# One more pair of token tiles through Strassen's algorithm in the output projection of a fused attention and gated feed-forward kernel

## Chip, cores and metric

The kernel runs on one core of one Trainium2 chip. The metric is the device time of one launch in microseconds (us), as the median of several runs; lower is better. TensorE is written PE (its weight loads PEld), VectorE DVE, ScalarE ACT, GpSimd POOL, and SyncE SP, which here only issues DMAs.

## What is computed

Windowed attention with a few global keys and a linear bias, then a feed-forward layer with a ReLU gate. Cut to what matters:

```python
scores = q @ k.T / sqrt(64) - slope[h] * dist        # 4 batches, 8 heads, 768 tokens, head size 64
a = softmax(where(is_global | is_local, scores, -1e9))    # 8 global keys, a window of 96
x = (a @ v)                                          # as 3072 tokens x 512
h = maximum(x @ w_gate, 0) * (x @ w_val)             # 512 -> 1536
out = h @ w_out                                      # 1536 -> 512, float32
```

## The kernel before

The 3072 tokens are worked in eight halves of 384 (a half is half a batch), numbered c = 0 to 7. A half's 384 tokens are three tiles of 128. For each half there are three kinds of work:

- **Attention** (`attention_pieces`): score matmuls into four PSUM banks at a time (`score_unit`, L513), the exponential on ACT (`unit_exp`, L522), a product with a mask table on DVE (L534, es times m_all, both bf16 in SBUF; it is emitted one piece later than its exponential, or at the next `flush`), the product with the values on PE (`piece_av`, L431, once for each of two heads of a pair: e = 0 and e = 1), then on ACT a logarithm (L440) and after the second head an exponential (L445) that make the reciprocal of the row sum, and on DVE a multiplication for each head that writes the normalised result to xT (`piece_norm`, L451). `N` below is the second of these two multiplications.
- **First projections** (`gate` and `val` in `ffn_pieces`): for each of 12 blocks of 128 hidden columns four matmuls of 128x384 with w_gate and four with w_val (both L741). ACT applies the ReLU to the gate's bank (L750), and DVE multiplies the val bank by it and writes ht, in fp16 (L757).
- **Output projection**: either `single(n)`, a tile by itself in four parts of three matmuls 128x512 with the weights wo_sb (`outp`, L774), with a copy to obuf on ACT (L779) and a store from SP (L780); or a `Pair`: two tiles with Strassen's algorithm. A pair makes seven products of six matmuls 128x256 (L632) where two single tiles need 24 matmuls of 128x512. It needs four sums of ht blocks (`sums`, L625 to L628, DVE, written to hsum), four differences of wo_sb blocks in wo_sum (`weight_sums`, L598), which are made once for all pairs, a copy of 128x256 on ACT (L659), four additions on DVE from PSUM into obuf (L643), and two stores (L652).

A bank for gate, val, a single tile or a pair's products comes from one pool of three (`ff_psum`), handed out in turn: the matmuls of a bank wait until the reader of the bank three before it is done. Attention's banks come from two other pools.

Half 0 and half 1 start together. Their attention and the first two thirds of their hidden columns are worked in an order written out by hand. The stage that the change touches comes after it (L990 to L993). It is one list of steps: the last four gate and val blocks of half 0 (steps 1 to 8), the same of half 1 (steps 9 to 16), half 0's three tiles as singles (steps 17 to 28), half 1's third tile as a single with the four sums of its pair behind its four parts (steps 29 to 32), and half 1's pair in seven products named p1, p2, p4, p6, p5, p7, p3 (steps 33 to 39). `weave` walks through this list and puts other pieces between the steps. Each step counts 0.65, and a piece with a fraction f is emitted after the first step at which the steps so far have reached f times the total. `spread` gives a list of pieces equal distances between two fractions. Three lists are spread here: the attention of half 2 over 0.02 to 0.86, the early pieces of half 3 over 0.1 to 0.76 (casts of k and q on POOL, L367; transposes as DMAs from SP, L372; copies that order the keys on POOL), and the eight weight differences over 0.42 to 0.76. Every engine works through its own instructions in the order in which they were emitted.

From half 2 on, each half is a stage of its own with the next half's attention woven in, and its first two tiles are a pair. The weights w_out are loaded with one DMA from POOL's queue before the stage (L923).

Of the kernel before, what the change touches and what calls it, by code (L numbers as in the profile page):

```python
# [16 lines left out]
def kernel(  # L17
# [88 lines left out]
    def w_of(t, dc, fc):  # L106
        f = fc % GW
        return t[fc // GW][:, dc, f * 128 : (f + 1) * 128]
# [269 lines left out]
    def early_pieces(s):  # L378
        out = [(0.0, lambda p=p: piece_cast2(s, p, kc, ks_of)) for p in range(HP)]
        out += [(0.0, lambda n=n: piece_x(kNb[s % 2], kc[s % 2], n)) for n in range(NN)]  # L380
        out += [(0.0, lambda p=p: piece_cast2(s, p, qc, qs_of)) for p in range(HP)]
        out += [(0.0, lambda n=n: piece_x(qT2[s % 2], qc[s % 2], n)) for n in range(NN)]
        out += [(0.0, lambda p=p: piece_order(s, p)) for p in range(HP)]
        return out
# [156 lines left out]
    def attention_pieces(s):  # L541
        masks, units = [], []

        def flush():
            for f in masks:
                f()
            masks.clear()

        def scores(groups, pools):
            units.extend(score_unit(s, groups, list(pools)))  # L550

        def x(scored=None):
            ready = masks[:]
            masks.clear()
            if scored:
                scores(*scored)
            masks.append(unit_exp(s, *units.pop(0)))
            for f in ready:
                f()

        U = [([(0, 0), (0, 1)], (AVB, QKB, QKB, QKB)),
             ([(0, 2), (1, 0)], (AVB, QKB, QKB, QKB)),
             ([(1, 1), (1, 2)], (AVB, QKB, QKB, QKB))]
        X = lambda u=None: [(0.0, lambda: x(u))]
        AV = lambda p: [(0.0, lambda e=e: (flush(), piece_av(s, p, e))) for e in range(2)]
        N = lambda p: [(0.0, lambda: piece_norm(s, p, 1))]
        wait = [(0.0, lambda: None)]
        a0, a1 = AV(0), AV(1)

        return (X(U[0]) + X() + X() + X() + wait + X(U[1]) + X() + X() + a0[0:1] + X() + a0[1:2] + N(0) + wait  # L570
                + X(U[2]) + X() + a1[0:1] + X() + X() + a1[1:2] + N(1) + wait * 2 + AV(2) + N(2) + wait * 2
                + AV(3) + N(3))
# [11 lines left out]
    NP = N_FC // 2  # L584
# [8 lines left out]
    def weight_sums(i0, i1):  # L593
        b = lambda f, d: B(i0, i1, f, d)
        t = lambda n: T(n, i0, i1)
        for out_, x, y in ((t(1), b(0, 1), b(0, 0)), (t(2), b(1, 1), t(1)),
                           (t(4), b(1, 0), t(2)), (t(3), b(1, 1), b(0, 1))):
            yield lambda o=out_, x=x, y=y: nc.vector.tensor_tensor(o, x, y, op=ALU.subtract)  # L598
# [132 lines left out]
    def ffn_pieces(c):  # L731
        ht_of[c] = ht = ht_pool.tile([128, N_FC, QH], FP16, name="ht")
        st = {}
        pair = Pair((c, 0), (c, 1))
        first = {}

        def products(key, w, fc, d0, d1):
            if d0 == 0:
                st[key] = ff_psum.tile([128, 512], FP32, name="ff_ps")
            for dc in range(d0, d1):  # L740
                nc.tensor.matmul(st[key][:, 0:QH], lhsT=w_of(w, dc, fc), rhs=xT_of[c][:, dc, :],  # L741
                                 start=(dc == 0), stop=(dc == N_DC - 1))
            return st[key]

        def gate(fc, d0=0, d1=N_DC):
            psg = products(f"g{fc % 4}", wg, fc, d0, d1)
            if d1 < N_DC:
                return
            gr = gr_pool.tile([128, QH], BF16, name="grelu")
            nc.scalar.activation(gr, psg[:, 0:QH], AF.Relu, bias=0.0, scale=1.0)  # L750
            st["r", fc] = gr

        def val(fc, d0=0, d1=N_DC):
            psv = products("v", wv, fc, d0, d1)
            if d1 < N_DC:
                return
            nc.vector.tensor_tensor(ht[:, fc, :], psv[:, 0:QH], st["r", fc], op=ALU.mult)  # L757

            if c > 1 and 7 <= fc < N_FC - 1:
                if fc == 7:  # L760
                    first[0] = pair.sums(0, 4)
                first[0][fc - 7]()

        f1 = []
        for fc in range(N_FC):
            f1.append((0.65, lambda *d, fc=fc: gate(fc, *d)))
            f1.append((0.65, lambda *d, fc=fc: val(fc, *d)))

        def outp(n, part, after):
            if part == 0:  # L770
                st["o"] = ff_psum.tile([128, DM], FP32, name="ff_ps")
            ps2 = st["o"]
            for fc in range(part * NP // 2, (part + 1) * NP // 2):
                nc.tensor.matmul(ps2, lhsT=ht[:, fc, n * 128 : (n + 1) * 128], rhs=wo_sb[:, fc, :],  # L774
                                 start=(fc == 0), stop=(fc == N_FC - 1))
            if part == 3:
                osb = obuf[:, n_results[0] % 2, 0:2]
                n_results[0] += 1
                nc.scalar.copy(osb, ps2)  # L779
                nc.sync.dma_start(out=out_v[c, n], in_=osb)  # L780
            for f in after:
                f()

        def single(n, *after):
            after = after or ((),) * 4
            return [(0.65, lambda part=part: outp(n, part, after[part])) for part in range(4)]

        if c == 0:
            return f1, single(0) + single(1) + single(2)
        late = pair.sums(0 if c == 1 else 4, NP)  # L790
        if c == 1:
            return f1, single(2, *([f] for f in late)) + pair.items()
        if c < NHALF - 2:
            return f1, single(2, [], [], [], late[0:2]) + pair.items({"1": late[2:4]})
        if c == NHALF - 2:
            return f1, pair.items({"1": late[0:2], "2": late[2:4]})

        space = qTb[0].rearrange("d p e t -> d (p e t)").bitcast(FP16)
        across = Pair((c - 1, 2), (c, 2), space.rearrange("t (s c z) -> t s c z", s=4, c=NP))
        sums = across.sums(0, NP)  # L800
        return f1, (pair.items({"1": late[0:2], "2": late[2:4], "4": sums[0:1], "6": sums[1:2], "5": sums[2:4]})
                    + across.items(split=True))


    def spread(items, first, last):

        n = len(items)
        return [(first + (i + 0.5) / n * (last - first), f) for i, (_, f) in enumerate(items)]
# [17 lines left out]

    V, P, A = nc.vector, nc.gpsimd, nc.scalar
    f1_0, f2_0 = ffn_pieces(0)
    f1_1, f2_1 = ffn_pieces(1)
    G = [slice(2 * GW * i, 2 * GW * (i + 1)) for i in range(N_FC // GW)]  # L830
    F0 = [f for _, f in f1_0]
# [147 lines left out]
    def T2_piece(p):  # L979
# [10 lines left out]
    sums_wo = [(0.0, f) for i in (0, 3) for f in weight_sums(i, i + 3)]  # L990
    weave(f1_0[G[2]] + f1_1[G[2]] + f2_0 + f2_1,
          spread(attention_pieces(2), 0.02, 0.86), spread(early_pieces(3), 0.1, 0.76),
          spread(sums_wo, 0.42, 0.76))  # L993

    for c in range(2, NHALF):
        placed = []
        if c + 1 < NHALF:
            placed.append(spread(attention_pieces(c + 1), 0.0, 0.92 if c + 2 < NHALF else 0.87))
        if c + 2 < NHALF:
            load_qk(c + 2, 0, H)  # L1000
            load_v_half(c + 2)
            placed.append(spread(early_pieces(c + 2), 0.25, 0.75))
        f1, f2 = ffn_pieces(c)
        weave(f1 + f2, *placed)
# [35 lines left out]
```

The softmax here doesn't subtract the row's maximum and nothing guards it: scores larger than these inputs give would overflow.

## Time and profile before

| what | value |
|---|---|
| median of 7 runs | 239.17 us (238.59 to 239.9) |
| the profiled execution | 239.37 us, of which the span from the first to the last instruction is 237.6 us |
| PE busy over the span | 230.9 us (97%), granted clock 1.00 |
| DVE, ACT, POOL busy | 174.3 us, 149.3 us, 89.2 us |
| matmuls 128x384 (L741) | 768, mean 326 ns |
| matmuls 128x512 (L774) | 96, mean 378 ns |
| matmuls 128x256 (L632), all groups | 336, median 273 ns |
| the stage of the change | 46.63 to 75.95 us |

A matmul's duration holds its way through the array, and the next one starts before it ends; what a matmul takes from PE's time is the distance from one start to the next. The same holds in part for DVE and ACT, where a following instruction that waits for nothing starts some 0.08 us before the end of the one before. In a timeline a row gives the start, the time that the merged instructions take together, the engine, the line, what is written and read, and how many instructions the row merges; in brackets stands the idle time before it and what ended that.

### The profile page before, as it was taken

The page shows a single profiled execution, that of the slowest core. Times are in us where ns is not written, and L with a number is a line of the kernel's source. Part 1 is how long each engine was busy: PE and PEld are TensorE (multiplying, and loading weights), DVE is VectorE, ACT ScalarE, POOL GpSimd, SP SyncE. Part 2 cuts the span into 40 slices and gives each one's busy share as a digit, 9 for nine tenths or more (in the row PEclk, how much of TensorE's full clock was granted, in tenths as well). Part 3 has the DMA queues.
Part 4 walks back from the last instruction along what each step waited for, and adds up shares of the span by engine and source line. Part 5 has one row for each costly group of instructions (what it writes and reads, how often), then busy time and mean ns, then how long its engine had stood idle before and what let it go on. Part 6 is the DMA issues. An engine that isn't in the chain of part 4 may idle for free.

```text
span 237.6 us, 5381 instructions
## 1 busy us (share of the span) xinstructions
PE 230.9 (97%) x1967; PEld 152.8 (64%) x1967; DVE 174.3 (73%) x442; ACT 149.3 (63%) x324; POOL 89.2 (38%) x191
## 2 busy tenths in 40 slices
PE   8899999999999999999999999999999999999993
PEld 4675766656558566766658666675658566766682
DVE  6877767756778689486867879576876878864783
ACT  7999856577653787557764787547764787523300
POOL 8998904924295066402492063701550000000000
PEclk9999999999999999999999999999999999999999
DMA  6999999998369943919349666649431200020004
GB/s 180 193 174 185 205 277 267 169 102 261 79 189 122 286 130 90 97 59 296 68 73 126 195 192 89 62 84 289 104 70 44 91 0 0 3 88 0 3 8 170
DMA packets 70650, 30.42 MB, mean 128 GB/s; under 512 B 47744, under 2 KB 69248, under 8 KB 70624
## 3 DMA queue, kind: packets, MB, share of 16 engines
q0 software_dynamic: 34896, 10.27, 38.4%
q1 hardware_dynamic: 35728, 19.82, 29.2%
q8 instruction: 15, 0.25, 0.4%
q14 instruction: 11, 0.09, 0.1%
HBM read 28.38 MB, written 6.29 MB: 146 GB/s over the span
## 4 chain that ended last, share of the span: by engine, by line
PE 84%; POOL 7%; DMA 4%; issue 1%; DVE 1%; ACT 0%; DVEq 0%; POOLq 0%
PE ff_ps L741 50%; PE ff_ps L632 15%; PE ff_ps L774 9%; PE av_ps L431 6%; DMA wv<-in_moe_w_val_dram 4%; POOL vbuf L154 3%; PE av_ps L513 2%; PE qk_ps L513 2%; POOL kc L131 1%; POOL wg L171 1%; POOL qT L195 1%; PE qk_ps L299 1%; DVE xT L451 0%; POOL wv L171 0%; POOL vbuf L141 0%
## 5 line engine op out<-in xcount | busy, mean ns | idle before, releaser
L741 PE MATMUL ff_ps<-xT,wv 128*128 128x384 bf16 x384 | 77.9, 326 | 0.1
L741 PE MATMUL ff_ps<-xT,wg 128*128 128x384 bf16 x384 | 77.9, 326 | 0.0
L750 ACT ACTIVATE grelu<-ff_ps 128x384 bf16<-128x384 f32 x96 | 46.7, 489 | 48.0 <-PE ff_ps L741 34.8
L757 DVE TENSOR_TENSOR ht<-ff_ps,grelu 128x384 f16<-128x384 f32 x96 | 53.3, 556 | 27.1 <-PE ff_ps L741 23.4
L741 PEld LDWEIGHTS <-wv 128*128 128x128 bf16 x384 | 36.0, 98 | 23.9 <-issue 1.1
L741 PEld LDWEIGHTS <-wg 128*128 128x128 bf16 x384 | 36.3, 98 | 22.0 <-issue 0.7
L451 DVE TENSOR_TENSOR xT<-av_ps,rcp 64x384 bf16<-64x384 f32 x48 | 26.6, 555 | 20.9 <-ACT rcp L445 19.8
L440 ACT ACTIVATE lnd<-av_ps 64x384 f32<-64x384 f32 x48 | 23.3, 485 | 16.0 <-PE av_ps L431 15.2
L534 DVE TENSOR_TENSOR es<-es,m_all 128x432 bf16<-128x432 bf16 (+3 forms) x108 | 30.9, 329 | 0.7 <-ACT es L522 0.7
L367 POOL CAST kc<-ks 128x384 bf16<-128x384 f32 x20 | 10.0, 542 | 55.3 <-DMA ks<-in_k_dram 47.7
L522 ACT ACTIVATE es<-qk_ps 128x432 bf16<-128x432 f32 (+2 forms) x54 | 27.8, 531 | 0.1
L154 POOL DMA_DIRECT2D vbuf<-in_v_dram x29 | 24.7, 861 | 0.3 <-DVE ht L757 0.3
L774 PE MATMUL ff_ps<-wo_sb,ht 128*128 128x512 f16 x96 | 23.6, 378 | 0.0
L431 PEld LDWEIGHTS <-vbuf 128*128 128x128 bf16 x216 | 18.3, 98 | 6.6
L643 DVE TENSOR_TENSOR obuf<-ff_ps,obuf 128x512 f32<-128x512 f32 (+1 forms) x34 | 20.0, 594 | 3.1 <-PE ff_ps L632 0.8
L431 PE MATMUL av_ps<-es,vbuf 128*128 128x216 bf16 (+4 forms) x216 | 21.4, 226 | 0.0
L632 PEld LDWEIGHTS <-hsum 128*128 128x128 f16 x168 | 16.3, 98 | 1.8
L632 PEld LDWEIGHTS <-ht 128*128 128x128 f16 x144 | 13.8, 98 | 2.9 <-DVE ht L757 0.4
L632 PE MATMUL ff_ps<-wo_sum,hsum 128*128 128x256 f16 x126 | 14.9, 272 | 0.0
L774 PEld LDWEIGHTS <-ht 128*128 128x128 f16 x96 | 8.6, 97 | 8.0 <-issue 0.6
L445 ACT ACTIVATE rcp<-lnd 128x384 f32<-128x384 f32 x24 | 12.6, 523 | 0.8
L632 PE MATMUL ff_ps<-wo_sb,ht 128*128 128x256 f16 x96 | 12.1, 273 | 0.1
(130 smaller groups left out, 254.1 us busy)
## 6 DMA issues: line engine op xcount, KB each, us to landing
out_dram<-obuf SPq DMA_DIRECT2D x22, 256.0 KB
ks<-in_k_dram SPq DMA_DIRECT2D x5, 768.0 KB
qs<-in_q_dram SPq DMA_DIRECT2D x5, 768.0 KB
vbuf<-in_v_dram POOLq DMA_DIRECT2D x23, 120.0 KB, 4.7
wv<-in_moe_w_val_dram POOLq DMA_DIRECT2D x3, 512.0 KB, 10.0
wo_sb<-in_moe_w_out_dram POOLq DMA_DIRECT2D x1, 1536.0 KB, 21.1
wg<-in_moe_w_gate_dram POOLq DMA_DIRECT2D x2, 512.0 KB, 10.0
ks<-in_k_dram SPq DMA_DIRECT2D x4, 192.0 KB
```

Source lines behind the costliest of these rows:

```text
L154: nc.gpsimd.dma_start(out=v_dst(b, NG + r0, NG + r0 + n, j), in_=v[b, :, KT * j + r0 : KT * j + r0 + n, :].rearrange("h p d -> p h d"))
L431: nc.tensor.matmul(av3[:, :, a : a + w], lhsT=vb[:, j, z0 : z0 + 128], rhs=es[:, c : c + NN * w].rearrange("k (n p) -> k n p", n=NN), star ...
L440: nc.scalar.activation(ln[o0 : o0 + 64], av[d0 : d0 + 64, 0:QH], AF.Ln, bias=0.0, scale=1.0)
L451: nc.vector.tensor_tensor(xT_of[s][r, p, :], av_of[s, p, e][r, 0:QH], av_of[s, p, "r"][r], op=ALU.mult)
L522: nc.scalar.activation(es[:, 0:cols], ps[:, 0:cols], AF.Exp, bias=0.0, scale=scale)
L534: nc.vector.tensor_mul(e4, e4, mk)
L632: nc.tensor.matmul(ps[:, c0 : c0 + DH], lhsT=lhs(i), rhs=rhs(i), start=(i == 0), stop=(i == NP - 1), skip_group_check=True)
L643: add = lambda o, x, y: nc.vector.tensor_tensor(o, x, y, op=ALU.add)
L741: nc.tensor.matmul(st[key][:, 0:QH], lhsT=w_of(w, dc, fc), rhs=xT_of[c][:, dc, :], start=(dc == 0), stop=(dc == N_DC - 1))
L750: nc.scalar.activation(gr, psg[:, 0:QH], AF.Relu, bias=0.0, scale=1.0)
L757: nc.vector.tensor_tensor(ht[:, fc, :], psv[:, 0:QH], st["r", fc], op=ALU.mult)
L774: nc.tensor.matmul(ps2, lhsT=ht[:, fc, n * 128 : (n + 1) * 128], rhs=wo_sb[:, fc, :], start=(fc == 0), stop=(fc == N_FC - 1))
```

## The change

Half 0's first two tiles are now a pair as well. Its list of steps is its third tile as a single, with the four sums of the pair behind its four parts, and then the seven products. The weight differences that this pair needs are spread over 0.08 to 0.4 of the stage instead of 0.42 to 0.76, among the gate and val steps. The stage has 38 steps instead of 39. Nothing else is touched.

```diff
@@ ffn_pieces
-        if c == 0:
-            return f1, single(0) + single(1) + single(2)
-        late = pair.sums(0 if c == 1 else 4, NP)
-        if c == 1:
+        late = pair.sums(0 if c < 2 else 4, NP)
+        if c < 2:
             return f1, single(2, *([f] for f in late)) + pair.items()
@@ the stage of halves 0 and 1
     weave(f1_0[G[2]] + f1_1[G[2]] + f2_0 + f2_1,
           spread(attention_pieces(2), 0.02, 0.86), spread(early_pieces(3), 0.1, 0.76),
-          spread(sums_wo, 0.42, 0.76))
+          spread(sums_wo, 0.08, 0.4))
```

## Prediction

> **What bounds the kernel now.** I read the page first: which engine fills the span, and what the chain that ended last is made of.
>
> ```profile
> PE 230.9 (97%) x1967; PEld 152.8 (64%) x1967; DVE 174.3 (73%) x442; ACT 149.3 (63%) x324; POOL 89.2 (38%) x191
> ...
> PEclk9999999999999999999999999999999999999999
> ...
> PE 84%; POOL 7%; DMA 4%; issue 1%; DVE 1%; ACT 0%; DVEq 0%; POOLq 0%
> ```
>
> TensorE is the bound at full clock, and hardly anything else is on the chain after the start. So matmul time taken out is gained, unless PE has to wait. Next, the stage of the change, 46.63 to 75.95 us. PE's timeline gives the price of each kind of matmul:
>
> ```profile
> 58.08 0.81 PE L741 MATMUL ff_ps<-xT,wv 128*128 128x384 bf16 x4
> ...
> 59.36 1.47 PE L774 MATMUL ff_ps<-wo_sb,ht 128*128 128x512 f16 x6
> 60.66 0.42 PE L431 MATMUL av_ps<-es,vbuf 128*128 128x216 bf16 x4
> ...
> 71.37 1.47 PE L632 MATMUL ff_ps<-wo_sb,ht 128*128 128x256 f16 x12
> 72.67 0.82 PE L632 MATMUL ff_ps<-wo_sum,ht 128*128 128x256 f16 x6
> ...
> 75.95 0.81 PE L741 MATMUL ff_ps<-xT,wg 128*128 128x384 bf16 x4
> ```
>
> From start to start: six 128x512 take 1.30 us (0.217 each), twelve 128x256 take 1.30 (0.108 each), the 42 of a pair 71.37 to 75.95, or 4.58 (0.109 each). A gate or val step is 0.65 us, an av piece (L431) 0.28. The steps add up to the stage's 29.32 us, so PE has almost no gap in it. The DVE timeline of the stage shows how near the gaps are:
>
> ```profile
> 50.08 0.56 DVE L757 TENSOR_TENSOR ht<-ff_ps,grelu 128x384 f16<-128x384 f32 x1 [0.72 <-PE ff_ps L741]
> 50.55 0.67 DVE L534 TENSOR_TENSOR es<-es,m_all 128x432 bf16<-128x432 bf16 x2
> 51.38 0.56 DVE L757 TENSOR_TENSOR ht<-ff_ps,grelu 128x384 f16<-128x384 f32 x1 [0.16 <-PE ff_ps L741]
> ...
> 58.30 0.55 DVE L451 TENSOR_TENSOR xT<-av_ps,rcp 64x384 bf16<-64x384 f32 x1 [1.21 <-ACT rcp L445]
> 58.77 0.54 DVE L757 TENSOR_TENSOR ht<-ff_ps,grelu 128x384 f16<-128x384 f32 x1
> 59.33 0.56 DVE L451 TENSOR_TENSOR xT<-av_ps,rcp 64x384 bf16<-64x384 f32 x1
> 59.92 0.56 DVE L757 TENSOR_TENSOR ht<-ff_ps,grelu 128x384 f16<-128x384 f32 x1
> 60.39 0.51 DVE L534 TENSOR_TENSOR es<-es,m_all 128x432 bf16<-128x432 bf16 x1
> 60.83 0.55 DVE L598 TENSOR_TENSOR wo_sum<-wo_sb 128x768 f16<-128x768 f16 x1
> ```
>
> The ht at 58.77 is step 14's (half 1's third val block of four). It ends at 59.31, and step 17, the first output step, starts at 59.36: it takes the bank three further on, so it needs that very ht. This has 0.05 us of room already.
>
> **The change part by part.**
>
> *Matmuls.* 24 x 0.217 = 5.20 us go, 4.58 come: 0.62 us less PE work. The rest of the stage from step 17 on was 75.95 - 59.36 = 16.59 us and becomes 15.97, if nothing waits.
>
> *The eight differences move from behind step 17 into steps 4 to 15.* One lasts 0.55 us; behind each other they start 0.47 apart (70.95, 71.42, 71.89, 72.36 for one difference and three sums of ht, same shape). Between 50.08 and 57.60 DVE is busy 4.96 of 7.52 us, with none of them. Six now fall in there: 6 x 0.47 = 2.82 us into 2.56 us of room. By the fractions, DVE's order after ht of step 4 is: mask 2, difference 1, mask 3, ht of step 6, difference 2, mask 4, difference 3, ht of step 8, mask 5, difference 4, mask 6, ht of step 10, mask 7, difference 5, ht of step 12, difference 6, mask 8, first normalisation, difference 7, second normalisation, ht of step 14. The last pair matters most: 38 steps instead of 39 move the second normalisation (fraction 0.342) from behind step 14 to behind step 13, so it and difference 7 now stand ahead of step 14's ht.
>
> Starts, with 0.47 for an ht or a difference, 0.33 for a mask (0.35 for masks 5 and 6, which are two instructions each): ht 50.08, difference 1 50.88, ht of step 6 51.68, ht of step 8 53.42 (its bank is ready at 53.25, as before), ht of step 10 55.06, ht of step 12 56.33 (ready 56.13), difference 6 56.80, mask 8 57.27, first normalisation 57.60. Its reciprocal is ready by then: the second av piece comes after step 12, at 55.86 instead of 56.51, and the logarithm and the exponential end at about 57.4. Then difference 7 at 58.07 (0.47), second normalisation 58.64 (0.57, as 69.31 to 69.88), ht of step 14 at 59.23 (0.59, as 59.33 to 59.92), end 59.79; 0.06 us later PE can start (58.85 to 58.91 is the same step from DVE to PE): 59.85. PE would have been there at 59.31. Everything after it stands behind this wait on PE, so the whole rest of the kernel moves by it. DVE never idles in between, so no wait further up changes this end. Cheapest case: were the differences shorter, the reciprocal would still hold the chain at 57.46, which gives 59.71.
>
> *Contention with POOL.* From 56.77 on POOL runs eight casts, which hang on a load and not on this change:
>
> ```profile
> 56.77 2.04 POOL L367 CAST kc<-ks 128x384 bf16<-128x384 f32 x4 [7.59 <-PE ff_ps L741]
> 58.81 1.86 POOL L367 CAST qc<-qs 128x384 bf16<-128x384 f32 x4
> ```
>
> Difference 6, mask 8 and difference 7 fall into them; all three read two SBUF operands. The trace has no difference beside a cast, but masks beside casts, in a later stage:
>
> ```profile
> 165.43 0.70 DVE L534 TENSOR_TENSOR es<-es,m_all 128x432 bf16<-128x432 bf16 x1
> ...
> 167.00 0.63 DVE L534 TENSOR_TENSOR es<-es,m_all 128x432 bf16<-128x432 bf16 x1
> ```
>
> An undisturbed one takes 0.37. Five such masks beside casts took 0.51 (60.39), 0.49 (111.51), 0.42 (113.08), 0.70 and 0.63: 0.05 to 0.33 us more, 0.18 in the mean. A difference beside POOL's key copies took 0.82 instead of 0.55. The Trainium skill (SBUF — State Buffer, "Who interferes with whom") has a stricter rule that speaks against this change: a VectorE instruction with two SBUF inputs and a GpSimd instruction that reads SBUF exclude each other for a whole instruction. By it each of the three could lose a whole cast, 0.51 us: 1.53 together. By the rows it is 3 x 0.18 = 0.54. I take the rows' mean, since they are the same pair of operations, and keep 0.15 and 1.53 for the range; below nothing it can't go, as the casts and these instructions stay the same work. Step 17 then starts at 59.85 + 0.54 = 60.39, or 1.03 us later than before.
>
> *The sum.* 1.03 - 0.62 = +0.41 us.
>
> *What I cost at nothing.* ACT loses two copies of 0.58 and gains one of 0.35. DVE gains four sums (0.47 each) and four additions (three of 0.69, one of 0.42) behind step 17, and seven differences have left there, so it stays at some 14 of 16 us. Worked on in order, the last sum of ht is done near 64, and the first product that reads one ends near 66.2; the additions that free the bank for half 1's single end near 67.7, and it starts near 68.7. That is 1 us of cover; beyond it PE waits one for one. The differences read w_out: that load was issued at 25.74 and took 21.1 us, so it landed near 46.8, 4 us before the first of them. On SP two stores of 256 KB are replaced by two of the same size; one stands ahead of the q transposes instead of three among them. Those ended near 69 and are needed at 76.7. What SP or ACT might gain or lose there is off PE's path.
>
> The profiled execution took 239.37 us with its span of 237.60, 1.77 around it, and the median is 0.20 lower. The sum is a difference within the span; I put it on the median: 239.17 + 0.41 = 239.6.
>
> **Rivals.**
>
> 1. *The saving arrives whole.* DVE absorbs the differences, step 17 starts at 59.31: -0.05 - 0.62 gives 238.5. For it: DVE is idle a third of that window. Against it: the 0.05 us of room, and the second normalisation's new place, which delays step 14's ht even if the differences cost nothing. Chance 0.10.
> 2. *The port decides, and the kernel is slower.* Difference 6, mask 8 and difference 7 each lose 0.33 (the worst row) to 0.51 us (a whole cast), because instructions of 0.55 us back to back always meet the next cast. Step 17 starts at 60.84 to 61.38, +0.86 to +1.40: 240.0 to 240.6. It decides from 0.29 us lost per instruction on. For it: the row of 0.82 beside key copies, and the skill's rule. Against it: most rows of masks. Chance 0.27.
> 3. *The pair doesn't take less PE time*, because 256 wide matmuls are held by their weight loads (98 ns under 109): near 240.2. Half 1's pair at 0.109 each speaks against it. Chance 0.03.
>
> The forecast itself, a wait at step 17 between 0.40 and 1.3 us, gives -0.27 to +0.7 and has 0.60.
>
> **How the numbers follow.** Likeliest: 239.6. The low end, 238.8, lies just under the cheapest case of the forecast (239.17 - 0.27 = 238.9) and leaves out rival 1. The high end, 240.5, reaches through nearly all of rival 2. A measurement here tells about 0.3% (0.7 us) from no change. Faster by more: half of rival 1, 0.05. Slower by more: rivals 2 and 3, 0.30. Within: 0.65.
>
> **What would show it.** In the changed profile: 72 matmuls L774 and 378 L632; the differences between 50.9 and 60.4 us; DVE without an idle gap from 50 to 60; the ht ahead of the first L774 ending between 59.7 and 61.3, and before that L774 PE idle with DVE ht L757 as its releaser; L598 or L534 rows stretched beside L367; the stage ending at 76.4 (75.95 before). If the first L774 starts at 59.3, the DVE count is wrong. If PE waits instead for the additions at half 1's single or for the sums of ht, my 1 us of cover was wrong, and the time is above the forecast.

## The result and the profile after

The changed kernel takes 238.3 us (median of 13 runs, 237.91 to 239.34) against 239.19 us (32 runs, 238.59 to 240.06): a ratio of 0.996 [0.995, 0.9971], or 0.9 us less. The forecast was 239.6 with a range from 238.8. The time is that of rival 1, the saving that arrives whole (238.5), though not for the reason that rival 1 gave.

The page of the changed kernel, the engines' busy time, the granted clock and the chain's shares:

```profile
PE 229.5 (97%) x1985; PEld 154.2 (65%) x1985; DVE 177.4 (75%) x450; ACT 148.4 (63%) x323; POOL 89.1 (38%) x191
...
PEclk9999999999999999999999999999999999999999
...
PE 83%; POOL 7%; DMA 4%; DVE 2%; issue 1%; ACT 0%; POOLq 0%; DVEq 0%
```

PE is still the bound at full clock, with 1.4 us less work; DVE has 3.1 us more and still hardly stands on the chain. PE's timeline around the first output step (step 17), at half 1's single and at the stage's end (a row gives start, time, engine, line, what is written and read, count, and in brackets the wait ahead of it, if there is one):

```profile
57.28 0.81 PE L741 MATMUL ff_ps<-xT,wg 128*128 128x384 bf16 x4
57.93 0.81 PE L741 MATMUL ff_ps<-xT,wv 128*128 128x384 bf16 x4
58.67 0.26 PE L513 MATMUL av_ps<-qT,kT 64*128 64x216 bf16 x1
...
59.13 1.47 PE L774 MATMUL ff_ps<-wo_sb,ht 128*128 128x512 f16 x6
...
67.41 1.46 PE L774 MATMUL ff_ps<-wo_sb,ht 128*128 128x512 f16 x6
...
75.12 0.81 PE L741 MATMUL ff_ps<-xT,wg 128*128 128x384 bf16 x4
```

No row of the stage has a bracket: PE waits nowhere, neither at step 17 (59.13) nor at half 1's single (67.41). The stage runs from 46.48 to 75.12, 28.64 us against 29.32 before: 0.68 less. Rival 1 had 0.67. DVE's timeline beside it:

```profile
55.98 0.56 DVE L757 TENSOR_TENSOR ht<-ff_ps,grelu 128x384 f16<-128x384 f32 x1
56.45 0.55 DVE L598 TENSOR_TENSOR wo_sum<-wo_sb,wo_sum 128x768 f16<-128x768 f16 x1
56.92 0.68 DVE L534 TENSOR_TENSOR es<-es,m_all 128x432 bf16<-128x432 bf16 x1
57.52 0.54 DVE L451 TENSOR_TENSOR xT<-av_ps,rcp 64x384 bf16<-64x384 f32 x1
57.99 0.54 DVE L598 TENSOR_TENSOR wo_sum<-wo_sb,wo_sum 128x768 f16<-128x768 f16 x1
58.56 0.56 DVE L451 TENSOR_TENSOR xT<-av_ps,rcp 64x384 bf16<-64x384 f32 x1
59.15 0.56 DVE L757 TENSOR_TENSOR ht<-ff_ps,grelu 128x384 f16<-128x384 f32 x1
```

The order and the lack of gaps are as forecast, and the last row is step 14's ht: it starts at 59.15 and ends at 59.71. But PE started step 17 at 59.13, before that ht had begun. So step 17 does not wait for it. What frees its bank stands in ACT's timeline, the ReLU of step 15's gate, which ends at 58.62, 0.51 us ahead of PE:

```profile
58.13 0.49 ACT L750 ACTIVATE grelu<-ff_ps 128x384 bf16<-128x384 f32 x1 [0.52 <-PE ff_ps L741]
```

The bank lists of two kernels below (`PICKS`), which write out the changed kernel's own order but for one exchange each, say the same: in this stage steps 1 to 16 each take the bank of three requests back, step 17 that of two back (step 15), and the pair's first product after it that of four back (step 14). So the banks are not handed out in turn, as the description of the kernel before has it; why the pool chooses as it does is not shown.

### The profile page after: what moved, and what is told of

The parts are those of the page before. It is cut to its first block, busy times and chain, and to the rows that moved or that the text cites. A ratio compares the mean times of both kernels' runs of the same rounds, so it can differ in the third digit from the quotient of the medians.

```text
span 236.4 us, 5424 instructions
## 1 busy us (share of the span) xinstructions
PE 229.5 (97%) x1985; PEld 154.2 (65%) x1985; DVE 177.4 (75%) x450; ACT 148.4 (63%) x323; POOL 89.1 (38%) x191
## 4 chain that ended last, share of the span: by engine, by line
PE 83%; POOL 7%; DMA 4%; DVE 2%; issue 1%; ACT 0%; POOLq 0%; DVEq 0%
PE ff_ps L741 51%; PE ff_ps L632 16%; PE ff_ps L774 7%; PE av_ps L431 6%; DMA wv<-in_moe_w_val_dram 4%; POOL vbuf L154 3%; PE av_ps L513 2%; PE qk_ps L513 2%; POOL kc L131 1%; DVE obuf L643 1%; POOL wg L171 1%; POOL qT L195 1%; PE qk_ps L299 1%; DVE xT L451 0%; POOL wv L171 0%
## 5 line engine op out<-in xcount | busy, mean ns | idle before, releaser
L757 DVE TENSOR_TENSOR ht<-ff_ps,grelu 128x384 f16<-128x384 f32 x96 | 53.3, 556 | 25.5 <-PE ff_ps L741 23.2
L367 POOL CAST kc<-ks 128x384 bf16<-128x384 f32 x20 | 10.8, 584 | 56.0 <-DMA ks<-in_k_dram 56.0
L643 DVE TENSOR_TENSOR obuf<-ff_ps,obuf 128x512 f32<-128x512 f32 (+1 forms) x38 | 22.6, 597 | 2.4 <-issue 0.5
L632 PEld LDWEIGHTS <-hsum 128*128 128x128 f16 x192 | 18.4, 98 | 2.1
L774 PE MATMUL ff_ps<-wo_sb,ht 128*128 128x512 f16 x72 | 18.0, 378 | 0.0
L632 PEld LDWEIGHTS <-ht 128*128 128x128 f16 x162 | 15.4, 97 | 3.3 <-DVE ht L757 0.4
L632 PE MATMUL ff_ps<-wo_sum,hsum 128*128 128x256 f16 x144 | 17.2, 272 | 0.0
L632 PE MATMUL ff_ps<-wo_sb,ht 128*128 128x256 f16 x108 | 13.9, 272 | 0.1
L522 ACT ACTIVATE es<-av_ps 128x432 bf16<-128x432 f32 (+2 forms) x18 | 9.5, 527 | 2.7 <-PE qk_ps L513 1.8
```

What stands on the lines that cost most here:

```text
L522: nc.scalar.activation(es[:, 0:cols], ps[:, 0:cols], AF.Exp, bias=0.0, scale=scale)
L632: nc.tensor.matmul(ps[:, c0 : c0 + DH], lhsT=lhs(i), rhs=rhs(i), start=(i == 0), stop=(i == NP - 1), skip_group_check=True)
L643: add = lambda o, x, y: nc.vector.tensor_tensor(o, x, y, op=ALU.add)
```

## The experiments

The theory after the result: the saving of 0.67 us arrives because step 17 stands on step 15's bank, and DVE's lag, which came about as forecast, ends in a bank that is needed only at the pair's first product (62.00). The rival: the lag itself is harmless, or was smaller than it seems, whichever bank is taken.

**The bank that the forecast assumed.** The changed kernel with its banks from a written list, in which step 17 gets step 14's bank and the pair's first product that of step 15; nothing else differs.

```diff
-    ff_psum = ctx.enter_context(tc.tile_pool(name="ffps", bufs=3, space=bass.MemoryType.PSUM))
+    ff_banks = [ctx.enter_context(tc.tile_pool(name=f"ffps{i}", bufs=1, space=bass.MemoryType.PSUM)) for i in range(3)]
+    # tile() takes ff_banks[PICKS[n]] for the n-th request
```

> The experiment that the first one meant to be, with the bank exchanged at the right place: the changed kernel, but step 17, half 0's single tile, gets the bank that the ht of step 14 empties, and the step after the single gets the other. Theory A (VectorE fell behind as forecast, and only the bank's owner differs): the first L774 starts 0.06 us after the ht of step 14 ends, 59.77 instead of 59.13 on the changed kernel's clock, and the stage becomes 0.64 us longer, 29.3 instead of 28.64: 238.9 us, ratio to before 0.999. Theory B (the lag is made up within the stage): 238.3 us, 0.996.

PE's timeline of this kernel at step 17, then DVE's (its lines stand 11 further down, so L785 is L774, L768 is L757):

```profile
60.04 1.46 PE L785 MATMUL ff_ps<-wo_sb,ht 128*128 128x512 f16 x6 [0.57 <-DVE ht L768]
```

```profile
59.43 0.56 DVE L768 TENSOR_TENSOR ht<-ff_ps,grelu 128x384 f16<-128x384 f32 x1
```

Now PE waits, 0.57 us, for the ht that ends at 59.99, and starts 0.05 us after it. The stage takes 29.26 us (46.76 to 76.02), 0.62 more than the changed kernel's and 0.06 less than before: the pair's saving is eaten in the place and by the wait that the forecast named. The time is 239.06 us, ratio 0.9979 [0.9967, 0.9991]. The theory holds; the rival falls.

**The same in another stage.** Meant for step 17, this list instead changed the bank of the first output step of half 3, which then gets the bank of the val block three back.

> The changed kernel with one difference: the first output step of the stage (step 17, half 0's third tile) gets the PSUM bank of step 14's val block, which VectorE empties, instead of the bank of step 15's gate block, which ScalarE empties. Theory A (VectorE did fall behind as worked out, and the forecast's wait is missing only because step 17 doesn't have that bank): step 17's first matmul starts 0.06 us after the ht of step 14 ends, at 59.8 instead of 59.1, and all that follows moves by 0.6 us: 238.9 us, ratio to the kernel before 0.999. Theory B (the lag of VectorE would be made up again within the stage, whichever bank is used): no change from the changed kernel, 238.3 us, 0.996.

PE's timeline of this kernel:

```profile
119.68 0.81 PE L752 MATMUL ff_ps<-xT,wv 128*128 128x384 bf16 x4
121.00 0.81 PE L785 MATMUL ff_ps<-wo_sb,ht 128*128 128x512 f16 x3 [0.51 <-DVE ht L768]
```

The stage of the change is as in the changed kernel (28.65 us), and the expected wait is absent there, since that bank was not touched. Where the list did hit, a wait of 0.51 us appears that neither kernel has, and what follows is 0.58 us later. The ratio is 0.9975 [0.9965, 0.9985]. So it tells nothing on step 17, but it shows the same thing at another place: half 3's single tile starts without a wait on the bank that the pool gave it, and with one on the val block's bank.

**The differences alone.** The kernel before, with the eight differences at 0.08 to 0.4 and no new pair.

> The kernel before with only the second part of the change: the eight weight differences at 0.08 to 0.4 of the stage, half 0's tiles still singles. Theory A: the differences cost nothing where they now are and gained nothing by leaving where they were, so 239.2 us, ratio 1.000, with the stage at 29.3 us. Theory C (a part of the gain of 0.89 us beyond the 0.62 us of matmuls comes from moving the differences away from the crowded end of the stage): 238.9 to 239.0 us, ratio 0.999. The theory of the forecast, with the waiting bank three steps back, gives 239.2 to 239.7 here.

239.22 us against 239.27, ratio 1.0001 [0.9988, 1.0014]; the stage takes 29.33 us without a wait on PE. The move by itself costs nothing and brings nothing, so the gain comes with the pair. The run does not test the bank: without the pair's shorter list, step 14's ht still stands ahead of the second normalisation and ends at 59.13, just before PE's 59.17, so whichever bank step 17 takes, hardly anything would wait.

**The differences later.** The changed kernel with them at 0.3 to 0.55 of the stage.

> The changed kernel with the differences at 0.3 to 0.55 of the stage instead of 0.08 to 0.4, about as late as the pair's products allow (the last one of those that the third product reads comes two steps ahead of it). Theory A: now VectorE's lag meets someone who waits: the third product (p4) reads a difference that ends near 64.1 and it would start at 63.6, so PE waits 0.3 to 0.8 us: 238.6 to 239.1 us, ratio 0.998 to 1.000. Theory B (lags on VectorE are made up within the stage): 238.3 us, 0.996.

PE's timeline of this kernel at the first product that reads a difference, then DVE's:

```profile
66.94 0.49 PE L632 MATMUL ff_ps<-wo_sum,ht 128*128 128x256 f16 x3 [1.80 <-DVE wo_sum L598]
```

```profile
60.44 1.36 DVE L598 TENSOR_TENSOR wo_sum<-wo_sb,wo_sum 128x768 f16<-128x768 f16 x2
61.72 0.55 DVE L757 TENSOR_TENSOR ht<-ff_ps,grelu 128x384 f16<-128x384 f32 x1
62.18 0.83 DVE L598 TENSOR_TENSOR wo_sum<-wo_sb 128x768 f16<-128x768 f16 x1
...
66.34 0.55 DVE L598 TENSOR_TENSOR wo_sum<-wo_sb,wo_sum 128x768 f16<-128x768 f16 x1
```

241.3 us, ratio 1.0077 [1.0052, 1.0102]; the stage takes 30.88 us, 2.24 more than the changed kernel's. The wait comes where it was expected and is much larger: three differences beside POOL's casts are stretched (the first two rows of L598: 1.36 for two where two undisturbed ones take 1.02, and 0.83 for one of 0.55), which makes 0.6 us of the 2.8 by which the last difference is later than expected (66.89, not near 64.1). The rest I put down to the queue of sums, masks and ht blocks among which the differences stand; no run separates it. The changed kernel needs an early place for the differences.

**Each difference twice.** The changed kernel with sixteen differences in the same stretch, the second of each writing the same values again.

```diff
-          spread(sums_wo, 0.08, 0.4))
+          spread([x for x in sums_wo for _ in range(2)], 0.08, 0.4))
```

> The changed kernel with each of the eight differences computed twice in a row, in the same stretch of the stage: 8 more VectorE instructions of 0.55 us, started 0.46 apart, so 3.7 us more VectorE work in a stretch that has none idle. Theory A: the lag grows from about 0.6 us at step 14 to about 4 us; a val block's bank comes round again after three or four steps (2 to 2.6 us), so PE waits 1.5 to 3 us: 239.8 to 241.3 us, ratio 1.003 to 1.009. Theory B: at most 0.5 us, 238.8 us.

PE's waits in this kernel's stage, as its timeline has them:

```profile
55.70 0.27 PE L431 MATMUL av_ps<-es,vbuf 128*128 128x144 bf16 x2 [1.14 <-DVE es L534]
...
59.07 0.81 PE L741 MATMUL ff_ps<-xT,wg 128*128 128x384 bf16 x4 [0.22 <-ACT grelu L750]
60.11 0.81 PE L741 MATMUL ff_ps<-xT,wv 128*128 128x384 bf16 x4 [0.22 <-DVE ht L757]
62.71 0.26 PE L513 MATMUL av_ps<-qT,kT 64*128 64x216 bf16 x1 [1.79 <-DVE xT L451]
...
70.92 0.42 PE L431 MATMUL av_ps<-es,vbuf 128*128 128x216 bf16 x4 [1.17 <-DVE xT L451]
```

243.71 us, ratio 1.0184 [1.016, 1.0208]; the stage takes 33.94 us, 5.30 more than the changed kernel's, where 1.5 to 3 were expected. Eight differences more are 8 x 0.47 = 3.8 us of DVE work. The expectation reckoned with the val banks; the one wait for a val bank has 0.22 us of idle time, and 0.39 from start to start (59.07 to 60.11, where a step is 0.65). Most of the wait is for attention: a mask, and the normalisations, 4.1 us of idle time in three rows. So this stretch of DVE had room for one set of differences and not for a second.

**More pairs.** The changed kernel with the third tiles of halves 2 and 3, and of 4 and 5, as pairs too.

> The changed kernel with two more pairs: the third tiles of halves 2 and 3, and those of halves 4 and 5, are multiplied as a pair at the end of the later half's stage, as halves 6 and 7 do already. Each takes 24 matmuls of 128x512 for 42 of 128x256, 0.62 us less PE time, and puts four sums (0.47 us each) and four additions (0.69, one of 0.42) on VectorE, which is busy 20 of 27 us in these stages. Theory A (VectorE may lag as long as nobody waits for it, and here it has 7 us to spare): 238.3 - 1.24 = 237.1 us, ratio 0.991. Rival (additions and sums of two pairs in a row hold the banks, 14 steps in 9.2 us with 8 additions and the attention's normalisations): at least the gain is lost, 238.3 us or more, 0.996.

PE's timeline of this kernel at half 2's pair:

```profile
96.87 0.28 PE L632 MATMUL ff_ps<-wo_sb,ht 128*128 128x256 f16 x1 [0.54 <-DVE ht L757]
96.99 0.82 PE L632 MATMUL ff_ps<-wo_sum,ht 128*128 128x256 f16 x6
```

241.74 us, ratio 1.01 [1.0073, 1.0127]. PE waits in these stages for the last ht (2.2 us in four places) and for xT (0.9 in two). In the changed kernel half 2's single tile stands there, from 93.89 on, between the last val block and the pair, and its twelve matmuls are the cover under which DVE finishes the ht blocks. Without it PE gives back more than the pairs save. The rival's direction held, but not its reason: no wait of PE in these stages is for a bank that an addition empties.

**The changed kernel again.** Between the profiles of before and after lies more than the stage: 0.15 us ahead of it, and 0.39 from the last half's first product to the end (the tail). There one of DVE's last additions waits in the kernel before and not in the changed one. DVE's timelines, before, then after:

```profile
232.88 1.62 DVE L643 TENSOR_TENSOR obuf<-ff_ps,obuf 128x256 f32<-128x256 f32 x4 [0.47 <-DVE obuf L643]
```

```profile
230.37 2.99 DVE L643 TENSOR_TENSOR obuf<-ff_ps,obuf 128x512 f32<-128x512 f32 x6 [0.18 <-PE ff_ps L632]
```

> The changed kernel once more, for its ratio against the kernel before. Theory A (the whole -1.03 us of the two profiles is real: 0.68 in the stage of the change, 0.35 in the tail, where a DVE addition waits 0.47 us in the kernel before and not in this one): ratio 0.9957, about 1.03 us less. Rival (only the stage counts, the tail's wait is an accident of one profile): ratio 0.9972, 0.68 us less.

238.04 us (7 runs) against 239.42, ratio 0.9949 [0.9928, 0.9969]. Its stage takes 28.65 us, as before, while it begins 0.99 us later (47.47 for 46.48): the start-up differs from one execution to the next, so profiles are compared stage by stage. The upper ends of both intervals, 0.9971 and 0.9969, lie just under the 0.9972 that the stage alone would give.

**The tail's wait.** Three ideas of what the wait hangs on, each as an edit of the kernel before. First, which of the two result buffers the pair writes (`n_results = [1]`):

> The kernel before with the two result buffers exchanged (the first result goes to the second one), nothing else. In the two profiles of kernels without half 0's pair, the third last but one addition of the tail waits 0.47 us and the last store is that much later; in the four profiles with the pair it doesn't. Half 0's pair makes one result fewer, so every later result uses the other buffer. If that is the reason: the wait is gone here, 238.8 us, ratio 0.9985. If not: 239.2 us, 1.000, with the wait.

The wait stays (0.47), ratio 1.0006 [0.9993, 1.0019]: not the buffer. Then nine memsets of 128x2 on DVE in the last half, behind its ht blocks, into a buffer that nothing reads:

> The kernel before with nine memsets of 128x2 on VectorE behind ht products of the last half, where VectorE has idle time; the rest is the same. It gives VectorE's instruction stream the changed kernel's length ahead of the tail. If the tail's wait of 0.47 us hangs on the place in the instruction stream: it is gone, 238.8 us, ratio 0.9985. If not: 239.2 us, 1.000, with the wait.

The wait is gone, but the ratio is 1.0001 [0.9986, 1.0016]. Then the nine memsets in half 4, and eighteen in the last half:

> The kernel before with nine memsets of 128x2 on DVE in the stage of half 4, that is far ahead of the tail. Theory A (the tail's wait of 0.47 us hangs on where the instruction stands in DVE's stream, counted from the program's start): the wait is gone from the profile as with nine memsets in the last half, and if it is real time the ratio is 0.9985. Theory B (it hangs on what lies just ahead of it in the last half): the wait is there, ratio 1.0.

> The kernel before with eighteen memsets of 128x2 on DVE in the last half instead of nine. Theory A (the place in the stream decides, and recurs with some period): the wait may be back or stand at another instruction; if it falls on no instruction of the tail the time is 0.35 us below before (ratio 0.9985). Rival (memsets cost what the wait gave back): ratio 1.0 to 1.001 without the wait in the profile.

Ratios 1.0004 [0.9993, 1.0015] and 0.9999 [0.9985, 1.0013]; the wait is gone from both profiles. DVE's timeline with the nine memsets in half 4 (lines one further down):

```profile
231.12 2.99 DVE L644 TENSOR_TENSOR obuf<-ff_ps,obuf 128x512 f32<-128x512 f32 x6 [0.18 <-PE ff_ps L633]
```

So the wait goes with each of the changes tried that lengthen DVE's stream ahead of it, even far ahead, but taking it away does not shorten the timed runs. Put together, in us against before (the first three columns from one profile each; the timed change is the ratio less 1, times its kernel before, with its 95% interval):

| kernel | the stage | between it and the tail | the tail | timed change |
|---|---|---|---|---|
| after | -0.68 | +0.01 | -0.39 | -0.96 [-1.20, -0.69] |
| after again | -0.67 | 0.00 | -0.39 | -1.22 [-1.72, -0.74] |
| step 14's bank | -0.06 | +0.01 | -0.39 | -0.50 [-0.79, -0.22] |
| half 3's bank | -0.67 | +0.58 | -0.38 | -0.60 [-0.84, -0.36] |
| differences alone | +0.01 | +0.03 | 0.00 | +0.02 [-0.29, +0.33] |
| the other result buffer | -0.01 | +0.01 | 0.00 | +0.14 [-0.17, +0.45] |
| nine memsets, last half | 0.00 | 0.00 | -0.39 | +0.02 [-0.34, +0.38] |
| nine memsets, half 4 | -0.01 | +0.01 | -0.38 | +0.10 [-0.17, +0.36] |
| eighteen memsets | -0.01 | 0.00 | -0.38 | -0.02 [-0.36, +0.31] |
| differences later | +1.56 | +0.01 | -0.38 | +1.84 [+1.24, +2.44] |
| each difference twice | +4.62 | 0.00 | -0.39 | +4.40 [+3.83, +4.98] |
| third tiles paired | -0.68 | +3.13 | -0.37 | +2.39 [+1.75, +3.04] |

The first four kernels gain 0.3 to 0.6 us more in the timed runs than the first two columns give, and each interval leaves their sum out, if only just for the changed kernel itself (-0.67 against -0.69). The tail does not explain it: the three kernels with memsets lose the same 0.4 us in their profiles, and their intervals leave such a gain out. Of the last three, the first fits the sum without the tail, and the other two fit both. A start-up that differs from kernel to kernel would be another explanation; the timed runs don't show it, and one profile for each kernel is too few. The stage's 0.68 is shown by every profile in which the changed stage stands as it is; whether some 0.3 us more of the change is real, and from where, stays open.

## Why the prediction was wrong

**The step that failed** is the sentence on step 17: "it takes the bank three further on, so it needs that very ht". It takes the bank of two requests back, the gate's, which was free 0.51 us before PE came. With this, "0.05 us of room" was a coincidence of two times, 59.31 and 59.36, and the whole +1.03 us falls away: the trace of the changed kernel shows PE starting before the ht, and the kernel with the assumed bank shows the wait, 0.57 us. What stood against rival 1 stood on this step alone. The description of the kernel before makes the same mistake ("handed out in turn"); it holds for steps 1 to 16 and not for the step after them.

Rival 1 was right by luck: it had DVE absorb the differences, and DVE did not. The prediction's own sign would have misled as well: "If the first L774 starts at 59.3, the DVE count is wrong". It started at 59.13, that is 59.28 on the clock of before (the stage began 0.15 earlier), and the DVE count was near.

The profile of the kernel before held a warning. If banks were handed out in turn, every single tile behind val blocks would stand on the val block three back. In the kernel before, half 3's first output step in PE's timeline, then the ht of the val block three back in DVE's:

```profile
120.87 0.81 PE L741 MATMUL ff_ps<-xT,wv 128*128 128x384 bf16 x4
121.61 0.81 PE L774 MATMUL ff_ps<-wo_sb,ht 128*128 128x512 f16 x3
```

```profile
121.51 0.56 DVE L757 TENSOR_TENSOR ht<-ff_ps,grelu 128x384 f16<-128x384 f32 x1
```

PE starts at 121.61, and that ht ends at 122.07. The rule of turns is refuted there, in a row that the prediction did not use. Nor did PE's row at 59.36 have a bracket: nothing in the trace had said that it waits.

**What held.** The matmuls: 0.62 forecast; from step 17 on the stage takes 15.99 us for 16.59, 0.60 less. The other 0.08 of the 0.68 lies between step 16 and step 17 (57.93 to 59.13 after, 58.08 to 59.36 before). The score matmuls there started 0.83 us behind step 16 in the kernel before, 0.06 after the first normalisation had ended (58.85):

```profile
58.91 0.26 PE L513 MATMUL av_ps<-qT,kT 64*128 64x216 bf16 x1
```

In the changed kernel that normalisation ends at 58.06 and they start 0.74 behind step 16 (58.67). The kernel with the differences alone has 0.83 again, so this part seems to come with the shorter list, which puts attention one step earlier, and not with the differences. Rival 1's 0.05 was near it. DVE's order and its run without idle, and the second normalisation ahead of step 14's ht, which starts at 59.15, that is 59.30 on the clock of before; the forecast was 59.23 without contention and 59.77 with it. The cover behind step 17: PE has no wait at half 1's single or at the products. The pair takes its reckoned PE time, so rival 3 falls.

**Contention was too large**, 0.54 forecast, 0.30 measured, and fell on the other engine too. Of the three instructions beside the casts only mask 8 was stretched (0.68, pitch 0.60 for 0.30); the two differences took 0.55 and 0.54. Without this 0.30 the ht would have started at 59.00, so the chain itself was 0.23 shorter than my sum, mostly since masks follow each other at 0.30, not 0.33 to 0.35. Rival 2 had 0.33 to 0.51 for each of the three, and its port did not decide. The casts paid as well. POOL's timeline after, then DVE's beside the last casts:

```profile
56.55 2.80 POOL L367 CAST kc<-ks 128x384 bf16<-128x384 f32 x4 [7.50 <-DMA ks<-in_k_dram]
59.30 2.50 POOL L367 CAST qc<-qs 128x384 bf16<-128x384 f32 x4
```

```profile
59.63 0.58 DVE L598 TENSOR_TENSOR wo_sum<-wo_sb 128x768 f16<-128x768 f16 x1
...
60.60 0.83 DVE L625 TENSOR_TENSOR hsum<-ht 128x768 f16<-128x768 f16 x1
61.36 0.68 DVE L534 TENSOR_TENSOR es<-es,m_all 128x432 bf16<-128x432 bf16 x1
```

From the first cast's start to the last one's end (61.80) it is 5.25 us, 3.90 before: 1.35 us more for POOL, off PE's path, with three differences, two masks and one sum of ht beside them. These six lost 0.93 us against undisturbed ones (0.31 for each mask, 0.28 for the sum, 0.03 for one difference), 0.16 in the mean, near the forecast's 0.18; but ahead of step 14's ht stood only one that was hit.

The section of the Trainium skill that I weighed (SBUF — State Buffer, "Who interferes with whom") calls the lock between the two engines exclusive. My "for a whole instruction" went further than the page: it says this of VectorE's 2-port modes, and of a VectorE instruction with two SBUF inputs only that it contends with a GpSimd instruction that reads SBUF. It also says that the order of issue decides who blocks, so it did not promise that VectorE would be the one. A whole cast for each of the three would have been 1.53 us on DVE; it lost 0.30. This trace agrees that the two engines hinder each other, in both directions: the longest cast took 0.99 us instead of 0.50. Whether the order of issue decided here, no run tests.

**Had the bank been step 14's**, the forecast would have been 0.47 us too high in the stage (+0.41 against -0.06): 0.24 from contention (0.54 for 0.30) and 0.23 from the chain. The mechanism would have been right, but not the sign: the stage would have come out as long as before, not 0.41 us longer.

## What to carry to other kernels

A wait is read from a row that has one; that two times lie 0.05 us apart, or that buffers are "handed out in turn", is a guess until another place in the same trace shows the same dependency. The matmuls that an algorithm saves could be counted here to a few hundredths of a us from start-to-start distances (0.62 forecast, 0.60 measured), and they arrive where the engine that prepares the operands is early enough: the same eight differences cost nothing at 0.08 to 0.4 of the stage and 2.2 us at 0.3 to 0.55. A tile that looks like plain work may be the cover under which another engine catches up; take it out and its time comes back as a wait.

## What the runs showed that I had not expected

- Where both engines worked back to back, eight casts on POOL took 1.35 us longer, and the six instructions of DVE beside them with both operands in SBUF 0.93 us, 0.30 of it ahead of step 14's ht.
- A wait of 0.47 us in DVE's stream near the end of the kernel went with nine instructions put in 10 to 20 us or some 90 us earlier, and the timed runs did not follow it.
- The start-up varies by over 1 us between the profiled executions (the stage begins at 46.11 to 47.54; 46.48 and 47.47 for the changed kernel alone), more than the whole effect of this change.
